# Rounding two weight blocks in turns, attention tiles between token-mixing products, and a block product moved behind the next group's first

## The chip, the core and the metric

The kernel runs on one core of a Trainium2 chip. The metric is the device time of one execution in microseconds (us). The kernel before takes 807.48 us (median of 3 runs, 807.12 to 807.95). The profiled execution has a span of 805.8 us from its first to its last instruction, at a granted TensorE clock of 0.999. All times inside a profile count from the start of that span.

The engines: TensorE (PE; PEld is its loading of weights), VectorE (DVE), ScalarE (ACT), GpSimd (POOL), and SyncE (SP), which issues the DMAs.

## The reference

```python
# attention: q, k, v are (8 batches, 8 heads, 576 tokens, 64)
kv  = einsum('bhsd,bhse->bhde', k, v)
o   = einsum('bhsd,bhde->bhse', q, kv)
x   = o / sqrt(mean(o*o, -1) + 1e-6) * g_norm       # RMS norm per head
x   = x.transpose(0, 2, 1, 3).reshape(8, 576, 512)  # heads side by side
# mixer
h   = relu(x^T @ w_tok1) @ w_tok2      # token mixing, 576 -> 256 -> 576
u   = x + h^T
out = u + relu(u @ w_ch1) @ w_ch2      # channel mixing, 512 -> 1536 -> 512
```

The mixer's weights are 64-bit floats in HBM. The kernel reads each as two 32-bit words and makes a rounded 32-bit float of it on the chip.

## The kernel before

It works in stages. Attention goes by pairs of batches (four pairs). Token mixing of one pair shares a stage with attention of the next, and both share it with the rounding of the weights:

- `start`: attention of pair 0 and the first token-mixing products
- `middle`: token mixing of pair 0, attention of pair 1
- `steady`, twice: token mixing of pair 1 and attention of pair 2, then of 2 and 3
- `last`: token mixing of pair 3
- then channel mixing, in nine groups of 512 rows (the ninth gathers the remainders), as block products in which sums of blocks take the place of one product. The first group (`channel1_once`, `channel2_once`) has wide products; the others have narrow ones in an order by places.

**Rounding of a block.** A block is fetched by a DMA and converted by ScalarE; six VectorE steps then follow, each on the result of the one before. "Step" in this text is one of these seven, from the conversion on.

```python
scale:  activation(dst, hi, Copy, scale=2**-112)                     # ScalarE, reads raw
clamp:  tensor_scalar(dst, dst, TOP, -TOP, min, max)                 # VectorE from here on
shift:  tensor_scalar(bits, bits, 3, logical_shift_left)
sign:   scalar_tensor_tensor(bits, raw[..., 1], 0x80000000, bits, bitwise_and, bitwise_or)
power:  tensor_scalar(part, bits, 0xFF800000, bitwise_and)
lower:  scalar_tensor_tensor(part, raw[..., 0], 2**-52, part, mult, mult)   # last use of raw
both:   dst = dst + part

def block(n, loads, dst):
    ...
    def fetch():                           # four buffers for raw
        raw.append(stage.tile([P, n, 2], U32, name="raw", tag="raw", bufs=4))
        for o, i in loads(raw[0]):
            dma(o, i)
    ...
    return (fetch,) + decode(dst, turn)    # decode returns the seven steps
```

**Attention of a pair.** A set is two tiles of 128 tokens; sets 0 and 1 belong to the first batch, 2 and 3 to the second, and 4 is the remainder of 64 tokens of each. A set takes both buffers of the pool `o`, so the next set starts when its gains and squares have read them.

```python
kv(side, half):    k^T v into ps["kv"]              # TensorE
evict(side, half): copy(kvp[side]..., ps_kv)        # ScalarE (VectorE for pair 0)
attend(c):         q^T kv into two tiles of ps["o"] # TensorE, set c
gain(c, h):        x = ps_o * g                     # VectorE
square(c, h):      sq = Square(ps_o)                # ScalarE
total(c, h):       tensor_reduce(ms, sq)            # VectorE
mean, sqrt, invert                                  # VectorE, ScalarE, VectorE (4 small steps)
scale(c, t):       eight activations x *= inv       # ScalarE
scale_pool(c, t):  tensor_mul(x, x, inv)            # GpSimd
```

**Token mixing of a pair.** Products h (`tok1`) fill four buffers of the pool `h`; the remainder's products end them; four relus on ScalarE free them; then nine tiles u (`tok2`) follow. Some u tiles are seeded: ScalarE copies x into the PSUM tile first, the products add to it, and ScalarE copies the result back. The others are added to x by VectorE.

**The stages as lists.** Each word is one step, and the order of the words is the order of issue, engine by engine: `kv`, `e` (evict), `l` (load), `a` (attend), `g` (gain), `q` (square), `t` (total), `m`, `r`, `i` (mean, sqrt, invert), `s` (scale), `p` (scale_pool), `h`, `hr`, `u`, `z` (seed), `lq` (load q), `w` (a token weight block's steps), `f` (fetch); a number is so many steps of the stream of channel weights.

```python
def steady(n0, n1):
    return [
        "kv00 l00 e00 1 -s40", "h00 3", "kv01 l01 e01 1", "h01 3", f"a0 q00 g01 q01 g00 {n0}",
        "h10 1 t00 t01 2", "h11 4", "hr 2 z2", "a1 q10 g11 q11 g10 1", "kv10 l10 e10 t10 t11 m0 r0 1",
        "u0 i0 1", "kv11 l11 e11", "u1 1 s00", "u2 z4 1", "a2 q20 g21 q21 g20", "u3 s01 t20 t21",
        "u4 z6 1", "a4 q40 g41 q41 g40 lq0", "u5 s10 t40 t41 1", "a3 q30 g31 q31 g30 lq1",
        "u6 s11 t30 t31 m2 r2 1 i2 p20 p21 s30", f"u7 1 s31 {n1}", "u8 2"]
```

The stream of channel weights, block after block, with the next block's conversion beside a block's fifth VectorE step and the fetch of the fourth next beside its sixth:

```python
def stream(blocks, ahead=4):
    steps = [blocks[0][1]]
    for n, block in enumerate(blocks):
        steps += block[2:]
        for at, m, k in ((-2, n + 1, 1), (-1, n + ahead, 0)):
            if m < len(blocks):
                steps[at] = do(lambda *fs: [f() for f in fs], steps[at], blocks[m][k])
    return iter(steps)
```

**From the first group to the second.** The first group's last steps, in the order of issue, are products 1, 6, 2, 7, 5, 4, 3 of `channel2_once`. In the second group's first block the products 1 and 6 stand at places 0 and 3, and between them ScalarE copies the result of product 1 (`read_first`). Before, two products without use stand around product 1:

```python
fetch_x(1, 0)
fetch_x(1, 1)
for place in range(2):
    t = late["c"].tile([P, DM], F32, name="ps_c")
    step = do(matmul, t[:, :FQ], lhsT=w_ch1[:, 0, 0, :P], rhs=w_ch1[:, 0, 0], start=True, stop=True)
    put(place, step) if place else step()
```

Of the kernel before, what the change touches and what calls it, by code (L numbers as in the profile page):

```python
# [11 lines left out]
F32 = mybir.dt.float32  # L12
# [7 lines left out]
def kernel(  # L20
# [33 lines left out]
    P = 128  # L54
    B, S, DM = k.shape
# [11 lines left out]
    FQ = FH // 2  # L67
# [31 lines left out]
    w_ch1 = consts.tile([P, 4, 4, FQ], F32, name="w_ch1")  # L99
# [6 lines left out]
    def do(f, *a, **kw):  # L106
        return lambda: f(*a, **kw)

    late = {}
# [4 lines left out]
    def dma(o, i, engine=nc.sync):  # L114
        keep(engine.dma_start(o, i))  # L115
# [10 lines left out]
    def matmul(*a, **kw):  # L126
        keep(nc.tensor.matmul(*a, **kw))  # L127
# [436 lines left out]
    def fetch_x(g, i):  # L564

        if g < NG:
            if i == 0:
                xg[g] = late["xg"].tile([P, J, DM], F32, name="xg")
            dma(xg[g][:, ts(i, 2)], u_dram[g].rearrange("(t p) e -> p t e", p=P)[:, ts(i, 2)])
# [11 lines left out]
    blocks, blocks_dram = {}, {}  # L581
# [37 lines left out]
    def m_psum(shape, name):  # L619
        return late["m"].tile(shape, F32, name=name, tag="m")  # L620
# [82 lines left out]
    def channel2_once(g):  # L703

        shape = [P, 2, DH]
        x = xg[g]
        quarter = lambda i, j: x[:, 2 * i:2 * i + 2, ts(j, DH)]

        def product(n, ps, start, stop):
            for p in range(2):  # L710
                for s in range(NS):
                    matmul(ps[:, p], lhsT=late["once"][n - 1][:, s, p], rhs=w2_of(n)[:, s],
                           start=(start and p == 0 and s == 0), stop=stop,
                           skip_group_check=True)

        p1, p6, p7, p5 = (m_psum(shape, f"ps_w{n}") for n in (1, 6, 7, 5))
        t1, u2, u3 = (r_tile() for _ in range(3))

        def first():
            product(1, p1, True, False)  # L720
            copy(t1, p1)

        def sixth():
            product(6, p6, True, True)
            tensor_add(u2, p6, t1)

        def seventh():
            product(7, p7, True, False)
            tensor_add(u3, p7, u2)
            tensor_add(quarter(0, 1), quarter(0, 1), u2)  # L730
            tensor_add(quarter(1, 0), quarter(1, 0), u2)

        def fifth():
            product(5, p5, True, False)
            tensor_add(u3, p5, u3)
            tensor_add(quarter(1, 1), quarter(1, 1), u3)

        def second():
            product(2, p1, False, True)
            tensor_add(quarter(0, 0), p1, quarter(0, 0))  # L740

        def fourth():
            product(4, p7, False, True)
            tensor_add(quarter(1, 0), p7, quarter(1, 0))
            store(g, xg, 1)

        def third():
            product(3, p5, False, True)
            tensor_add(quarter(0, 1), p5, quarter(0, 1))
            store(g, xg, 0)  # L750

        return [first, sixth, second, seventh, fifth, fourth, third]
# [7 lines left out]
    def put(place, *steps):  # L760
        beside[place] += steps

    def outer(place, size, mul, to, base=None, act=copy, onto=False):

        banks, t = {}, {}

        def product(n, name, start, stop):
            if start:
                banks[name] = m_psum([P, size], f"ps_{name}")
            mul(n, banks[name], start, stop)

        def temp(n, bufs):
            t[n] = late["tmp"].tile([P, FQ], F32, name=n, tag=n, bufs=bufs)[:, :size]
            t[n] = fit(t[n])
            return t[n]

        def fit(flat):
            return flat if size == P else flat.rearrange("p (w t) -> p w t", w=W)

        def read(o, i, j):

            if base:
                tensor_add(o, fit(banks["a"]), base(i, j))
            else:
                copy(o, fit(banks["a"]))

        def read_first():
            banks["c"] = late["c"].tile([P, DM], F32, name="ps_c")[:, :size]
            read(fit(banks["c"]), 0, 0)

        def write(i, j, name, n):
            tensor_add(to(i, j), fit(banks[name]), to(i, j) if onto else t[n])

        def put_on(i, j, n):
            if onto:
                tensor_add(to(i, j), to(i, j), t[n])  # L800

        def take(i, j, name, act):
            if onto:
                tensor_add(to(i, j), banks[name], to(i, j))
            else:
                act(to(i, j), fit(banks[name]))

        def at(n, name, start, stop, *steps):
            def all_of():
                product(n, name, start, stop)  # L810
                for step in steps:
                    step()

            products[place + PLACE[n]] = all_of

        at(1, "a", True, False, read_first)
        at(6, "a", False, False, lambda: read(temp("u2", 2), 0, 1))
        at(5, "b", True, False)
        at(7, "a", False, False, lambda: read(temp("u3", 1), 1, 1))
        at(2, "c", False, True, lambda: take(0, 0, "c", act))  # L820
        put(place + PLACE[7] + (1 if onto else 2), do(put_on, 1, 1, "u3"), do(write, 1, 1, "b", "u3"))
        at(4, "a", False, True, lambda: take(1, 0, "a", copy) if onto else read(to(1, 0), 1, 0))
        put(place + PLACE[4], do(put_on, 0, 1, "u2"))
        at(3, "b", False, True)
        put(place + PLACE[3] + 1, do(write, 0, 1, "b", "u2"))
# [213 lines left out]
    def weave(body, fill):  # L1039
        done = 0  # L1040
        for n, step in enumerate(body):
            step()
            upto = len(fill) * (n + 1) // len(body)
            while done < upto:
                fill[done]()
                done += 1

    def stream(blocks, ahead=4):


        steps = [blocks[0][1]]
        for n, block in enumerate(blocks):
            steps += block[2:]
            for at, m, k in ((-2, n + 1, 1), (-1, n + ahead, 0)):
                if m < len(blocks):
                    steps[at] = do(lambda *fs: [f() for f in fs], steps[at], blocks[m][k])
        return iter(steps)

    def play(lines, after={}, **stages):
# [38 lines left out]
    for block in tok1[2:] + tok2:  # L1098
# [5 lines left out]


    start = [
        "kv00 e00 l00 j14 w01 w11 w02 w03 w04 w05 w06 w07 w12 w13 w14 w15 w16 w17", "kv01 j10 e01 l01 f0",
        "a00 g00 q00", "a01 g01 q01 t00", "a10 g10 q10 t01 m0 r0", "a11 g11 q11 t10 i0 p00 p01",
        "kv10 j6 t11 m1 r1 e10 i1 s10 p11", "kv11 j2 e11", "h000 h001 h002 h003", "a20 g20 q20", "a21 g21 q21 t20",
        "h010 t21 m2 r2", "a30 g30 q30 i2 p20", "a31 g31 q31 t30", "h011 t31 m3 r3 p21", "a40 i3 p30 g40 q40 p31",  # L1110
        "h012 h013 t40 m4 r4 w21 i4 s40 lq0 l10 l11"]
    middle = [
        "kv00 e00 w31 w22 w23 w24", "h10 w25 w26 w27 f1 -lq1 l00 w32 w33 w34", "kv01 e01 l01 w41 w35 w36 w37",
        "h11 f2 w42 w43 w44", "hr w45 w46 w47 f3", "a0 q00 g01 q01 g00 t00 t01", "u0 z2 1", "u1 1",
        "a1 q10 g11 q11 g10 t10 t11 m0 r0", "u2 i0 1", "kv10 e10 z4 s00", "u3 1 s01", "kv11 e11 1",
        "u4 1 z6", "a2 q20 g21 q21 g20 s10", "u5 t20 t21 2", "a4 q40 g41 q41 g40 lq0 l10 l11", "u6 t40 t41 2",
        "a3 q30 g31 q31 g30 lq1 s11", "u7 t30 t31 m2 r2 1 i2 p20 p21 s30", "u8 1 s31"]

    def steady(n0, n1):
        return [  # L1120
            "kv00 l00 e00 1 -s40", "h00 3", "kv01 l01 e01 1", "h01 3", f"a0 q00 g01 q01 g00 {n0}",
            "h10 1 t00 t01 2", "h11 4", "hr 2 z2", "a1 q10 g11 q11 g10 1", "kv10 l10 e10 t10 t11 m0 r0 1",
            "u0 i0 1", "kv11 l11 e11", "u1 1 s00", "u2 z4 1", "a2 q20 g21 q21 g20", "u3 s01 t20 t21",
            "u4 z6 1", "a4 q40 g41 q41 g40 lq0", "u5 s10 t40 t41 1", "a3 q30 g31 q31 g30 lq1",
            "u6 s11 t30 t31 m2 r2 1 i2 p20 p21 s30", f"u7 1 s31 {n1}", "u8 2"]

    attentions = [attention(0, ((0,), (1,), (2,), (3,), (4,)))]
# [28 lines left out]
    first = ExitStack()  # L1156
# [47 lines left out]
    n = len(sums1) // 3  # L1204
# [8 lines left out]
             lambda: [f() for f in outer_u(1)], lambda: [f() for f in inner_u(1, 0, 7)]]  # L1213
    extra += [lambda: None] * (len(channel2_once_steps := channel2_once(0)) - len(extra))
    body = [step for pair in zip(channel2_once_steps, extra) for step in pair]
    weave(body, lasts + [f for fs, _ in inner2 for f in fs] + [f for _, f in inner1])
    fetch_x(1, 0)
    fetch_x(1, 1)


    for place in range(2):
        t = late["c"].tile([P, DM], F32, name="ps_c")
        step = do(matmul, t[:, :FQ], lhsT=w_ch1[:, 0, 0, :P], rhs=w_ch1[:, 0, 0], start=True, stop=True)
        put(place, step) if place else step()
    for n, (_, f) in enumerate(inner2):
        put(8 + n, f)
    for g in range(1, NG):
# [42 lines left out]
```

## Time and profile before

| Part of the profiled execution | number |
|---|---|
| span | 805.8 us |
| PE busy, share of the span | 788.6 us, 98% |
| PEld | 694.4 us, 86% |
| DVE | 683.3 us, 85% |
| ACT | 302.2 us, 38% |
| POOL | 79.6 us, 10% |
| DMA, mean over the span | 218 GB/s |
| first channel product (`ps_v`) starts | 200.17 us |
| second group's first product (`ps_a`) starts | 273.44 us |

A busy share is an average over stages with different limits, and the ends of matmuls are modelled, so a busy PE isn't PE at its peak. What a change is worth is read in the stage that it touches: which gaps the engine has there that sets the end, and what ended each of them. In the timeline, a number in brackets is the idle time before an instruction, with the engine and the tile that released it. Every product of 32-bit floats shows as two records in the profile, so a u tile of two products is "x4". Tiles are named for what they hold: `ps_o` and `ps_r` are sets and the remainder, `ps_h` and `ps_u` token mixing, `sq` squares, `raw` the fetched words, `w_ch` and `w_tok` weights.

### The profile page before, as it was taken

What the parts mean: (1) busy time and instruction counts of PE and PEld (TensorE: products, weight loads), DVE (VectorE), ACT (ScalarE), POOL (GpSimd) and SP (SyncE); (2) the same over time, 40 slices, a digit from 0 to 9 for tenths busy, and PEclk for the clock granted to TensorE, in tenths of its full rate; (3) what the DMA queues carried; (4) which work ended last, traced back from release to release, by engine and by line L of the source; (5) the groups of instructions that cost most, each with busy time, mean ns of one, the idle gap of its engine ahead of it and who ended that gap; (6) DMA issues with size and microseconds to landing.
All of it is one profiled execution on the core that took longest, in us unless ns stands there. A gap on an engine that the chain in (4) does not pass through costs nothing.

```text
span 805.8 us, 17651 instructions
## 1 busy us (share of the span) xinstructions
PE 788.6 (98%) x7012; PEld 694.4 (86%) x7012; DVE 683.3 (85%) x1308; ACT 302.2 (38%) x838; POOL 79.6 (10%) x75
## 2 busy tenths in 40 slices
PE   6999999999999999999999999999999999999997
PEld 6645554544888899999999999999999999999997
DVE  4688989999886978978987997997898899799687
ACT  1357585664110134234234234332424423423331
POOL 1210101010000011012003003001101200300300
PEclk9999999999999999999999999999999999999999
DMA  9999998436458567468467648738836855863642
GB/s 289 320 345 351 334 354 304 158 119 208 150 175 294 194 210 239 131 221 267 149 201 240 201 153 259 234 118 262 265 119 217 262 166 181 250 201 123 218 147 83
DMA packets 97346, 175.51 MB, mean 218 GB/s; under 512 B 7024, under 2 KB 54128, under 8 KB 97264
## 3 DMA queue, kind: packets, MB, share of 16 engines
q1 hardware_dynamic: 95584, 172.65, 66.6%
q10 hardware_dynamic: 1680, 1.74, 0.7%
q8 instruction: 55, 0.90, 0.5%
q14 instruction: 27, 0.22, 0.1%
HBM read 137.79 MB, written 36.57 MB: 216 GB/s over the span
## 4 chain that ended last, share of the span: by engine, by line
PE 83%; DVE 6%; DMA 5%; ACT 3%; SPq 1%; issue 1%; ACTq 0%; DVEq 0%
PE ps_a L127 37%; PE ps_b L127 19%; PE ps_c L127 9%; PE ps_v L127 5%; PE ps_w L127 4%; PE ps_u L127 4%; DMA v_in<-in_v_dram 3%; PE ps_h L127 2%; ACT x L475 1%; SPq L115 1%; DMA raw<-in_moe_w_ch_dram 1%; DMA k_in<-in_k_dram 1%; DVE ms L442 1%; DVE part L187 1%; DVE x L421 1%; PE ps_o L127 1%
## 5 line engine op out<-in xcount | busy, mean ns | idle before, releaser
L124 ACT COPY u<-ps_a 128x128 f32<-128x128 f32 (+1 forms) x160 | 56.1, 351 | 156.6 <-PE ps_a L127 156.6
L118 POOL TENSOR_TENSOR v<-v,v 128x384 f32<-128x384 f32 (+1 forms) x48 | 61.4, 1301 | 532.8 <-ACT v L124 492.8
L127 PE MATMUL ps_b<-uT,sums 128*128 128x128 f32 x672 | 86.2, 276 | 0.0
L127 PEld LDWEIGHTS ps_b<-uT,sums 128*128 128x128 f32 x672 | 80.7, 192 | 0.2
L118 DVE TENSOR_TENSOR v<-v,v 128x768 f32<-128x768 f32 (+1 forms) x86 | 79.5, 932 | 1.1
L127 PE MATMUL ps_a<-uT,w_ch 128*128 128x128 f32 x576 | 78.9, 275 | 0.0
L124 ACT COPY ps_c<-ps_a 128x128 f32<-128x128 f32 (+1 forms) x80 | 26.9, 336 | 129.5 <-PE ps_a L127 129.5
L118 DVE TENSOR_TENSOR v<-ps_b,u 128x384 f32<-128x384 f32 x112 | 61.5, 549 | 12.3 <-PE ps_b L127 10.6
L127 PEld LDWEIGHTS ps_a<-uT,w_ch 128*128 128x128 f32 x576 | 71.4, 192 | 0.4
L127 PE MATMUL ps_u<-h,w_tok 128*128 128x512 f32 (+1 forms) x160 | 68.0, 608 | 1.6 <-ACT h L121 0.6
L127 PE MATMUL ps_h<-x,w_tok 128*128 128x512 f32 (+1 forms) x160 | 65.9, 604 | 0.0
L118 DVE TENSOR_TENSOR uT<-uT 128x512 f32<-128x512 f32 (+4 forms) x103 | 63.1, 629 | 0.8
L127 PE MATMUL ps_a<-uT,w 128*128 128x128 f32 x432 | 60.0, 275 | 0.0
L127 PEld LDWEIGHTS ps_a<-uT,w 128*128 128x128 f32 x432 | 54.0, 192 | 0.0
L127 PEld LDWEIGHTS ps_h<-x,w_tok 128*128 128x128 f32 (+1 forms) x160 | 25.9, 189 | 31.1 <-issue 28.3
L127 PEld LDWEIGHTS ps_u<-h,w_tok 128*128 128x128 f32 (+1 forms) x160 | 24.5, 178 | 31.9 <-issue 24.9
L121 ACT ACTIVATE v<-v 128x384 f32<-128x384 f32 (+1 forms) x86 | 42.5, 528 | 23.0 <-DVE v L118 22.5
L118 DVE TENSOR_TENSOR sv<-v 128x384 f32<-128x384 f32 x80 | 43.4, 551 | 8.9 <-ACT v L121 8.9
L118 DVE TENSOR_TENSOR xg<-xg,r 128x512 f32<-128x512 f32 x74 | 50.0, 686 | 0.7
L475 ACT ACTIVATE x<-x,inv 128x64 f32<-128x64 f32 x184 | 46.0, 336 | 9.6 <-DVE inv L461 9.6
L127 PE MATMUL ps_a<-sums,sv 128*128 128x128 f32 x336 | 47.1, 276 | 0.0
L127 PE MATMUL ps_a<-uT,sums 128*128 128x128 f32 x336 | 46.8, 275 | 0.0
(134 smaller groups left out, 1576.5 us busy)
## 6 DMA issues: line engine op xcount, KB each, us to landing
sums<-sums SPq DMA_DIRECT2D x112, 576.0 KB, 4.4
qT<-in_q_dram SPq DMA_DIRECT2D x8, 1152.0 KB, 9.6
xt<-u_dram SPq DMA_DIRECT2D x36, 256.0 KB, 4.0
blocks<-y SPq DMA_DIRECT2D x72, 128.0 KB, 2.7
uT<-blocks SPq DMA_DIRECT2D x36, 256.0 KB, 4.9
xg<-u_dram SPq DMA_DIRECT2D x18, 512.0 KB, 5.1
k_in<-in_k_dram SPq DMA_DIRECT2D x16, 512.0 KB, 9.2
u_dram<-x SPq DMA_DIRECT2D x16, 512.0 KB, 4.9
```

What stands on the lines that cost most here:

```text
L115: keep(engine.dma_start(o, i))
L118: keep(engine.tensor_tensor(out=o, in0=a, in1=b, op=op))
L121: keep(nc.scalar.activation(o, a, AF.Relu))
L124: keep(nc.scalar.copy(o, a))
L127: keep(nc.tensor.matmul(*a, **kw))
L187: keep(nc.vector.scalar_tensor_tensor(out=part[0], in0=raw()[..., 0], scalar=2.0 ** -52, in1=part[0], op0=ALU.mult, op1=ALU.mult))
L421: keep(nc.vector.tensor_mul(x, bank[c, h], g_sb.to_broadcast([P, number(c), D])))
L442: keep(nc.vector.tensor_reduce(stats_of(c)[0][:, h], sq[c, h], axis=AX.X, op=ALU.add))
L475: keep(nc.scalar.activation(x[:, k, h], x[:, k, h], AF.Copy, scale=inv[:, k, h]))
```

## The change

It has three parts. Rounding goes through two blocks in turns: three steps of one block alternate with three of the block before, so that neighbours don't depend on each other, and the conversions and fetches get other places. In the steady stages, the second set of attention moves from behind the h products to between them; the tiles u and the remainder are regrouped, and the seeds and scalings move with them. Then the first group's last block product moves behind the second group's first product, in the place of the two products without use, and two of the first group's four PSUM tiles come from another pool.

```diff
-        p1, p6, p7, p5 = (m_psum(shape, f"ps_w{n}") for n in (1, 6, 7, 5))
+        p1, p6 = (m_psum(shape, f"ps_w{n}") for n in (1, 6))
+        p7, p5 = (late["c"].tile(shape, F32, name="ps_c", tag="c") for _ in range(2))
@@
-            banks["c"] = late["c"].tile([P, DM], F32, name="ps_c")[:, :size]
+            banks["c"] = late["c"].tile([P, DM], F32, name="ps_c", tag="c")[:, :size]
@@ def stream(blocks, ahead=4):
+        def all_of(*fs):
+            return do(lambda: [f() for f in fs])
         steps = [blocks[0][1]]
-        for n, block in enumerate(blocks):
-            steps += block[2:]
-            for at, m, k in ((-2, n + 1, 1), (-1, n + ahead, 0)):
-                if m < len(blocks):
-                    steps[at] = do(lambda *fs: [f() for f in fs], steps[at], blocks[m][k])
+        second = [None] * 3
+        for n in range(len(blocks) + 1):
+            first = list(blocks[n][2:5]) if n < len(blocks) else [None] * 3
+            if n + 1 < len(blocks):
+                first[1] = all_of(first[1], blocks[n + 1][1])
+            if second[1] and n - 1 + ahead < len(blocks):
+                second[1] = all_of(second[1], blocks[n - 1 + ahead][0])
+            steps += [f for pair in zip(first, second) for f in pair if f]
+            second = list(blocks[n][5:8]) if n < len(blocks) else second
         return iter(steps)
@@ start
-        "kv00 e00 l00 j14 w01 w11 w02 w03 w04 w05 w06 w07 w12 w13 w14 w15 w16 w17", "kv01 j10 e01 l01 f0",
+        "kv00 e00 l00 j14 w01 w11 w02 w03 w04 w12 w05 w13 w06 w14 w07 w15 w16 w17", "kv01 j10 e01 l01 f0",
@@ middle
-        "kv00 e00 w31 w22 w23 w24", "h10 w25 w26 w27 f1 -lq1 l00 w32 w33 w34", "kv01 e01 l01 w41 w35 w36 w37",
-        "h11 f2 w42 w43 w44", "hr w45 w46 w47 f3", "a0 q00 g01 q01 g00 t00 t01", "u0 z2 1", "u1 1",
-        "a1 q10 g11 q11 g10 t10 t11 m0 r0", "u2 i0 1", "kv10 e10 z4 s00", "u3 1 s01", "kv11 e11 1",
-        "u4 1 z6", "a2 q20 g21 q21 g20 s10", "u5 t20 t21 2", "a4 q40 g41 q41 g40 lq0 l10 l11", "u6 t40 t41 2",
-        "a3 q30 g31 q31 g30 lq1 s11", "u7 t30 t31 m2 r2 1 i2 p20 p21 s30", "u8 1 s31"]
+        "kv00 e00 w31 w22 w23 w24", "h10 w41 w25 w32 w26 w33 w27 w34 f1 -lq1 l00", "kv01 e01 l01 w35 w42 w36 w43",
+        "h11 w37 w44 f2", "hr w45 w46 w47 f3", "a0 q00 g01 q01 g00 t00 t01", "u0 z2 1", "u1 1",
+        "a1 q10 g11 q11 g10 t10 t11 m0 r0", "u2 i0 1", "kv10 e10 z4 s00 p10", "u3 1 s01", "kv11 e11 z6 1",
+        "u4", "a2 q20 g21 q21 g20 s11", "u5 t20 t21 1", "a4 q40 g41 q41 g40 lq0 l10 l11", "u6 t40 t41 3",
+        "a3 q30 g31 q31 g30 lq1", "u7 t30 t31 m2 r2 2 i2 p20 p21 s30", "u8 1 s31"]
@@ def steady(n0, n1):
-            "h10 1 t00 t01 2", "h11 4", "hr 2 z2", "a1 q10 g11 q11 g10 1", "kv10 l10 e10 t10 t11 m0 r0 1",
-            "u0 i0 1", "kv11 l11 e11", "u1 1 s00", "u2 z4 1", "a2 q20 g21 q21 g20", "u3 s01 t20 t21",
-            "u4 z6 1", "a4 q40 g41 q41 g40 lq0", "u5 s10 t40 t41 1", "a3 q30 g31 q31 g30 lq1",
+            "h10 t00 t01 3", "a1 q10 g11 q11 g10", "h11 t10 t11 m0 r0 3", "hr i0 2",
+            "kv10 l10 e10 1", "kv11 l11 e11 z2", "u0 s00 1", "u1 2", "a2 q20 g21 q21 g20", "u2 s01 z4 t20 t21 1",
+            "u3 1", "a4 q40 g41 q41 g40 lq0", "u4 s10 t40 t41 z6 1", "u5 1", "a3 q30 g31 q31 g30 lq1",
@@ first group to second
     body = [step for pair in zip(channel2_once_steps, extra) for step in pair]
+    behind = body.pop(-2)
     weave(body, lasts + [f for fs, _ in inner2 for f in fs] + [f for _, f in inner1])
-    fetch_x(1, 0)
-    fetch_x(1, 1)
-    for place in range(2):
-        t = late["c"].tile([P, DM], F32, name="ps_c")
-        step = do(matmul, t[:, :FQ], lhsT=w_ch1[:, 0, 0, :P], rhs=w_ch1[:, 0, 0], start=True, stop=True)
-        put(place, step) if place else step()
+    put(0, behind, do(fetch_x, 1, 0), do(fetch_x, 1, 1))
```

## The prediction

> **What bounds the kernel now.** I read the busy lines first, then the engines by windows, then the timelines of single engines around each gap of TensorE. The windows give start and end in us, length, then busy us (and instructions) of PE, PEld, DVE, ACT and POOL, the clock, the DMA share and GB/s:
>
> ```profile
> 80.00:100.00 20.00, 20.00 (x220) 10.02 (x216) 19.34 (x28) 9.77 (x31) 2.79 (x2) 1.00 1.08 336
> 180.00:200.00 20.00, 20.00 (x54) 7.92 (x52) 19.73 (x24) 9.17 (x17) 0.00 (x0) 1.00 0.64 197
> 300.00:500.00 200.00, 200.00 (x1790) 199.93 (x1789) 173.07 (x353) 69.58 (x194) 23.39 (x19) 1.00 0.66 207
> ```
>
> Behind 200 us, three quarters of the span, TensorE is packed (the answer on waits names none for PE behind 290 us), so all that comes before it shifts the end one for one. In the attention and token mixing stages, up to 200 us, TensorE and VectorE are both nearly full, and up to 137 us the DMA is too (37.38 MB from 30 to 140 us, 340 GB/s). The change can earn only TensorE's gaps. The timeline of TensorE shows the four largest ones of the stages that are changed; the number in brackets is the idle time and what ended it:
>
> ```profile
> 54.75 2.81 PE L127 MATMUL ps_u<-h,w_tok 128*128 128x512 f32 x6 [0.55 <-DVE w_tok L118]
> ...
> 74.24 1.16 PE L127 MATMUL ps_o<-kvp,qT 64*64 64x64 f32 x64 [1.33 <-ACT sq L425]
> ...
> 101.97 1.98 PE L127 MATMUL ps_u<-h,w_tok 128*128 128x512 f32 x4 [0.57 <-ACT h L121]
> ...
> 161.93 1.16 PE L127 MATMUL ps_o<-kvp,qT 64*64 64x64 f32 x64 [1.12 <-ACT sq L425]
> ```
>
> With small ones (0.04, 0.21, 0.2, 0.26, 0.1) all gaps from 54 us on sum to 4.4 us. The kernel's first TensorE instruction of each pair's stage (kv00) starts at 40.18 (middle), 79.01 (steady one), 123.38 (steady two), and the last stage at 168.52 us.
>
> The timeline of VectorE shows what a dependence costs. Columns: start, duration:
>
> ```profile
> 96.46 0.55 DVE L166 TENSOR_SCALAR w_ch<-w_ch 128x768 f32<-128x768 f32 x1
> 97.05 0.56 DVE L170 TENSOR_SCALAR w_ch<-w_ch 128x768 uint32<-128x768 uint32 x1
> ...
> 101.10 0.55 DVE L166 TENSOR_SCALAR w_ch<-w_ch 128x768 f32<-128x768 f32 x1
> 101.57 0.68 DVE L421 TENSOR_TENSOR x<-ps_o,g_sb 128x512 f32<-128x512 f32 x1
> ```
>
> The same clamp holds VectorE 0.59 us when the next one reads its result, 0.47 when it doesn't: 0.12 us for each neighbouring pair of dependent steps.
>
> [...] the last rounding step takes 1.70 us at 83.19, beside GpSimd's scaling (81.28 to 84.07), and 0.96 elsewhere. [...]
>
> **The change, part by part.**
>
> *Rounding in turns.* Each stage of a pair has some 15 neighbouring dependent pairs before (counted in the timeline from 123 to 168 us) and next to none after: 15 x 0.12 = 1.8 us of VectorE in each steady stage, 9 x 0.12 = 1.1 in the last. No PE gap is VectorE's throughput as such, so this only shortens lags. For the token weights (44 to 54.6 us) the interleave gains under 0.2 us: VectorE's first step of the next block stands before the old block's last two and must wait for ScalarE (46.95 us).
>
> *Price: raw words are needed earlier.* Fetch of a block stays at nearly the same step, but its first conversion (ScalarE) moves 5 steps forward. In before the sixth block already stalls ScalarE. Its timeline:
>
> ```profile
> 91.39 0.92 ACT L163 ACTIVATE w_ch<-raw 128x768 f32<-128x768 f32 x1
> 100.00 0.94 ACT L163 ACTIVATE w_ch<-raw 128x768 f32<-128x768 f32 x1 [7.70 <-DMA raw<-in_moe_w_ch_dram]
> 100.84 2.05 ACT L121 ACTIVATE h<-ps_h 128x512 f32<-128x512 f32 x4
> ```
>
> The DMA is full and the same bytes are queued ahead of that block, so I expect it at about 100 us again.
>
> *Middle.* One rounding step less (0.9 us) stands ahead of the remainder tile's gains, and the third set's wait of 1.33 goes; but a conversion (0.8 us) now stands ahead of the eviction that the second side's first set needs, so that set starts some 0.7 late. One scaling (eight ScalarE instructions, 1.9 us) goes to GpSimd, about 1 us there by the rows at 37.44 and 40.91 (two in 2.04), which only lightens ScalarE where TensorE doesn't wait for it. By its steps this stage ends 0.7 to 0.8 us earlier: steady one begins at 78.2.
>
> *Steady one.* From 78.2, by TensorE's own times (kv 1.3, h 3.63, set 1.09, h with remainder 5.35), the second set now stands between two h products, at 92.7 to 93.8, and TensorE reaches the first u at 101.7. But ScalarE now has the sixth block's conversion ahead of that set's squares, and the relus behind those. From 100.0: conversion 0.84, first square 0.6, gain 0.6, two reductions 1.2, mean 0.1 and turn 0.1, root 0.2, two relus 1.1: u can start at 104.8, a wait of **3.1 us**. The second kv product, worth 1.3, is done by then, and was not before.
> VectorE, stopped from 96.7 to 101.4, is late for the third set (ends 109.5): its gains end 3.1 us after it. ScalarE's second square waits for the first gain, then copy 0.48, eight scalings 1.92 and the seed 0.48 stand before u4; TensorE has only two u tiles and the remainder (4.3 us) meanwhile: wait 3.1 + 0.5 + 2.9 - 4.3 = **2.2**. From 104.8: u 3.63, set 1.09, u 3.63, remainder 0.65, wait 2.2, u 3.63, set 1.09, u 5.4: 126.2, against 123.38.
>
> *Steady two.* DMA is no longer full. The set that waited 1.12 now has two u tiles ahead of it: that wait goes, and 0.36 of small ones. VectorE's lag at the third set comes to 2.4, so the seed of u4 makes TensorE wait 2.4 + 0.5 + 2.9 - 4.3 = 1.5. Of work alone the stage is 42.9, so it takes 44.4 against 45.2: the last stage begins at 170.6 against 168.6, **+2.0**. There TensorE works 31.6 us without waits; VectorE's 1.1 keep it ahead.
>
> *Boundary to the second group.* Timeline of TensorE and its weight loads:
>
> ```profile
> 272.79 0.81 PE L127 MATMUL ps_c<-w_ch 128*128 128x384 f32 x2
> ...
> 274.11 0.81 PE L127 MATMUL ps_c<-w_ch 128*128 128x384 f32 x2
> ...
> 274.82 0.74 PEld L127 LDWEIGHTS ps_a<-uT,sums 128*128 128x128 f32 x6 [0.52 <-ACT ps_c L124]
> ```
>
> The two products only fill time, 0.65 and 0.71 us; both go. The block product of 5.13 us covers the copy that they covered. But that copy needs a buffer whose last reader on VectorE ends at 272.7 before and some 0.5 later now: about 0.3 back here, 0.3 at the next block: **-0.8**.
>
> Sum: +2.0 - 0.8 = +1.2, so 808.7 if the sixth block lands at 100 us and all queues go as above.
>
> **Rivals.** *The raw words don't stop it.* If they came 4 us earlier, u would start at 101.8, VectorE's lag would be 1.4 and the seed's wait 0.5: steady one ends at 121.5, steady two gives 0.8, the boundary 0.8: -3.5, so 804.0. For it: the change takes the waits one by one as if tuned to a trace. Against: the bytes ahead are the same, and the DMA share is 1.08.
> *VectorE is what counts.* If the lags drop more than I count (1.8 us a stage), the waits on seeds vanish: another 2 to 3 us less, toward 802 to 803 with the first rival. Against: VectorE itself waited for ScalarE or TensorE in the same stages.
> *Nothing moves.* The gaps close, open again elsewhere, and only the boundary's 0.8 stay: 806.7.
>
> **Range and chances.** I give the stall seven chances in ten (about +1.2, give or take 1.5) and the rivals three (-1 to -4.5). I put the point a little below the stall's sum: 808.0, eight in ten from 803.6 to 810.0. All gaps together are 4.4 + 1.4 = 5.8 us, 0.7%, so a gain of over 2% can't come from here, and a loss of 16 us would need waits five times what I count.
>
> **What would show it.** In the timeline of ScalarE after, a conversion released by the raw DMA near 100 us, the second set's squares behind it; in that of TensorE a wait of about 3 us at the first u of steady one on the relus, waits of 1 to 2 us on seeds (ps_u on ACT) near 114 and 158, none on squares at the last set; kv00 of steady two near 126, block product next to ps_a without filler near 268 to 274. If ScalarE never waits for raw near 90 to 100, my sum is wrong by 4 us and the first rival holds. If steady two starts before 123, it fell.

## The result, and the profile after

The changed kernel takes 811.0 us (median; 810.49 to 811.27) against 807.3 of the kernel before (806.82 to 807.95): a ratio of 1.0045, 95% interval 1.0027 to 1.0062. It is slower by 3.7 us where 808.0 was predicted, and lies outside the range of 803.6 to 810.0. The profiled executions show 808.7 against 805.8 us, of which 3.9 us are lost before 200 us (the first channel product starts at 204.08 instead of 200.17) and 1.0 won back behind it.

The timeline of TensorE in the changed kernel, its larger gaps and the first kv product of each steady stage (start, duration, and in brackets the idle time before with what ended it):

```profile
73.88 1.16 PE L127 MATMUL ps_o<-kvp,qT 64*64 64x64 f32 x64 [0.71 <-ACT sq L425]
...
78.66 1.33 PE L127 MATMUL ps_kv<-v_in,k_in 128*64 128x64 f32 x40
...
89.34 0.93 PE L127 MATMUL ps_o<-kvp,qT 64*64 64x64 f32 x48 [0.39 <-ACT kvp L124]
...
105.24 5.32 PE L127 MATMUL ps_u<-h,w_tok 128*128 128x512 f32 x8 [2.22 <-ACT h L121]
...
116.77 3.70 PE L127 MATMUL ps_u<-h,w_tok 128*128 128x512 f32 x8 [0.86 <-ACT ps_u L124]
...
127.28 1.33 PE L127 MATMUL ps_kv<-v_in,k_in 128*64 128x64 f32 x40
...
161.83 3.70 PE L127 MATMUL ps_u<-h,w_tok 128*128 128x512 f32 x8 [1.81 <-ACT ps_u L124]
```

Left out are 0.26 at 67.80 (set 2 on a kv eviction) and 0.32 at 121.88 and 166.94 (the seeds of u6). The gaps from 54 us on now sum to 7.4 us, against 4.0 by the same count before. The predicted waits are there: the first u on the relus, the seed of u4 in both steady stages, none on squares in steady two. In middle, where the wait on squares was to go, 0.71 of it stayed. Compare the durations, too: eight u records take 3.70 us at 116.77 and **5.32 at 105.24**. The windows of the same stretch say why. Behind the busy times (and instructions) of PE, PEld, DVE, ACT and POOL their last three numbers are the granted clock, the DMA share and GB/s; the third from the end is the one to read.

```profile
104.00:105.00 1.00, 0.00 (x0) 0.00 (x0) 1.00 (x2) 1.00 (x3) 0.00 (x0) 1.00 1.08 428
105.00:106.00 1.00, 0.76 (x1) 0.50 (x2) 1.00 (x2) 1.00 (x3) 0.00 (x0) 0.56 0.96 372
106.00:107.00 1.00, 1.00 (x2) 0.33 (x1) 0.90 (x5) 1.00 (x4) 0.00 (x0) 0.50 1.00 368
...
108.00:109.00 1.00, 1.00 (x3) 0.49 (x2) 1.00 (x3) 1.00 (x6) 0.00 (x0) 0.73 1.09 326
```

TensorE idles for 2.2 us, and then its granted clock is half for more than 3 us (0.56, 0.50, 0.50 and 0.73 in the four windows from 105 to 109 us). That was in no step of the prediction. The mean clock of the whole span, 0.998, hides it (the kernel before has 0.999).

The cause of the idle time stands in the timeline of ScalarE, and one engine further in that of VectorE:

```profile
100.42 0.92 ACT L163 ACTIVATE w_ch<-raw 128x768 f32<-128x768 f32 x1 [8.67 <-DMA raw<-in_moe_w_ch_dram]
101.24 1.07 ACT L425 ACTIVATE sq<-ps_o 128x512 f32<-128x512 f32 x2
103.99 0.23 ACT L452 ACTIVATE root<-ms 128x32 f32<-128x32 f32 x1 [1.68 <-DVE ms L447]
104.12 2.04 ACT L121 ACTIVATE h<-ps_h 128x512 f32<-128x512 f32 x4
```

```profile
101.86 0.69 DVE L421 TENSOR_TENSOR x<-ps_o,g_sb 128x512 f32<-128x512 f32 x1 [4.36 <-ACT sq L425]
102.47 1.27 DVE L442 TENSOR_REDUCE ms<-sq 128x8 f32<-128x512 f32 x2
```

The sixth block's conversion waits for its raw words until 100.42; set 1's squares, the gain that they release, two reductions, the root and the relus follow one after another, and TensorE comes last. This is the predicted chain, link by link; only the wait at its end, 2.22 us, is shorter than the 3.1 worked out, because TensorE reached u at 103.0 and not at 101.7.

At the boundary to the second group (timeline of TensorE) the product stands where it was meant to, at the small price of a wait of 0.23:

```profile
271.53 0.83 PE L127 MATMUL ps_a<-uT,w_ch 128*128 128x128 f32 x6
272.19 5.35 PE L127 MATMUL ps_c<-w_ch,v 128*128 128x256 f32 x24
277.77 0.94 PE L127 MATMUL ps_a<-uT,sums 128*128 128x128 f32 x6 [0.23 <-ACT ps_c L124]
```

### The profile page after: what moved, and what is told of

It reads as the page before. It is cut to its first block, busy times and chain, and to the rows that moved or that the text cites. A ratio compares the mean times of both kernels' runs of the same rounds, so it can differ in the third digit from the quotient of the medians.

```text
span 808.7 us, 17645 instructions
## 1 busy us (share of the span) xinstructions
PE 788.1 (97%) x7008; PEld 694.0 (86%) x7008; DVE 678.6 (84%) x1308; ACT 300.2 (37%) x830; POOL 80.3 (10%) x76
## 4 chain that ended last, share of the span: by engine, by line
PE 84%; DVE 7%; ACT 4%; DMA 3%; issue 1%; SPq 1%; ACTq 0%; DVEq 0%
PE ps_a L127 37%; PE ps_b L127 19%; PE ps_c L127 10%; PE ps_u L127 5%; PE ps_v L127 5%; PE ps_h L127 4%; ACT x L475 2%; PE ps_w L127 2%; DVE x L421 1%; DVE ms L442 1%; DMA raw<-in_moe_w_ch_dram 1%; PE ps_kv L127 1%; PE ps_o L127 1%; DMA k_in<-in_k_dram 1%; PE ps_j L127 1%
## 5 line engine op out<-in xcount | busy, mean ns | idle before, releaser
L127 PE MATMUL ps_a<-sums,v 128*128 128x128 f32 x336 | 46.7, 275 | 0.0
```

## The experiments

Fifteen kernels were compared, counting before and after; each of the others was timed in five rounds beside the kernel before, whose median was 807.1 to 807.5.

| Kernel | what it is | us | ratio to before (95%) |
|---|---|---|---|
| bound | before + boundary | 806.47 | 0.9989 (0.9982 to 0.9996) |
| turns | before + rounding in turns, start, middle | 813.44 | 1.0072 (1.0059 to 1.0085) |
| sets | before + new steady lists | 809.78 | 1.0024 (1.0015 to 1.0033) |
| conv6 | after, sixth conversion later | 807.60 | 1.0005 (0.9996 to 1.0015) |
| fetch6 | after, sixth fetch ahead of k and v | 807.60 | 1.0008 (1.0000 to 1.0016) |
| warm | after + products in the wait | 811.00 | 1.0048 (1.0036 to 1.0060) |
| seeds | after, seeds ahead of scalings | 805.89 | 0.9985 (0.9978 to 0.9991) |
| seedswarm | seeds + products in the wait | 805.97 | 0.9982 (0.9973 to 0.9991) |
| early | conv6 + seeds | 803.34 | 0.9957 (0.9945 to 0.9969) |
| plain | early without rounding in turns | 803.71 | 0.9961 (0.9949 to 0.9974) |
| early2 | early + kv evictions earlier | 803.88 | 0.9964 (0.9950 to 0.9979) |
| early3 | early + seventh conversion later | 803.83 | 0.9957 (0.9944 to 0.9971) |
| early4 | early3 + kv evictions earlier | **802.48** | 0.9945 (0.9932 to 0.9957) |

### The three parts by themselves

```diff
# bound: of the change's diff, the hunks on p7, p5, tag="c" and "first group to second"
# turns: of the change's diff, the hunks on stream, start and middle
# sets:  of the change's diff, the hunk on steady
```

> The kernel before with the third part of the change alone: the first group's last block product behind the next group's first, the two products without use gone, two PSUM tiles from the other pool. Theory R (the loss comes from the sixth weight block's conversion, which stops ScalarE in steady one): this part gains what I counted, 0.8 us, so some 806.5 us. Rival P (the moved product or the smaller pool costs): 808 us or more.

Measured: −1.0 us, as theory R and the prediction's last step have it. Rival P is out: the boundary is no part of the loss.

> The kernel before with rounding in turns and the new lists of start and middle, but with its own lists of the steady stages and its own boundary. The sixth conversion again waits for its raw words until about 100 us, but here the relus and not set 1's squares stand behind it. Theory R: the first u waits about 1 us on relus instead of 0.57, TensorE's clock stays up, and what middle gains (0.35) pays for it: 807 to 808 us. Rival V (the order of the sets costs, whatever rounding does): the same 807. Rival F (rounding in turns costs by itself, by its fetches and conversions everywhere): 810 or more.

Measured: 813.44, over 5 us more than theory R allowed. The timeline of ScalarE in turns shows what I had missed:

```profile
99.66 0.91 ACT L163 ACTIVATE w_ch<-raw 128x768 f32<-128x768 f32 x1 [7.91 <-DMA raw<-in_moe_w_ch_dram]
...
105.31 0.90 ACT L163 ACTIVATE w_ch<-raw 128x768 f32<-128x768 f32 x1 [2.79 <-DMA raw<-in_moe_w_ch_dram]
...
107.60 0.26 ACT L124 COPY kvp<-ps_kv 128x128 f32<-128x128 f32 x1
110.25 0.23 ACT L452 ACTIVATE root<-ms 128x32 f32<-128x32 f32 x1 [2.39 <-DVE ms L447]
110.38 0.25 ACT L124 COPY kvp<-ps_kv 128x128 f32<-128x128 f32 x1
```

The sixth conversion waits, with only the relus behind it, and TensorE waits for nothing there. But the *seventh* waits as well, and in the old lists a seed, set 1's squares, the root and both kv evictions stand behind it; the second eviction starts at 110.38, where the kernel before has it at 106.67. TensorE then waits for a kv eviction and for a seed (timeline of TensorE in turns):

```profile
110.68 0.93 PE L127 MATMUL ps_o<-kvp,qT 64*64 64x64 f32 x48 [1.56 <-ACT kvp L124]
...
115.83 2.44 PE L127 MATMUL ps_u<-h,w_tok 128*128 128x512 f32 x4 [2.12 <-ACT ps_u L124]
```

and behind that the granted clock falls to 0.50 (118 to 120 us): its four u records take 2.44 instead of 1.98. So the mechanism holds, but not for one block alone: here the seventh conversion, moved forward, stops what stands behind it on ScalarE. Rival F, that rounding in turns costs by its conversions, named the size better than I did.

> The kernel before with the new lists of the steady stages alone: the second set between the h products, the seeds behind the scalings, rounding one block after another. The sixth conversion stands five steps later, behind set 1's squares. Theory R: no wait above 1 us at the first u of steady one and no lower clock there; the seeds of u4 cost about 1 us in each steady stage, the wait of 1.12 before the last set goes: 807 to 808 us. Rival V: 810 or more, without rounding in turns.

Measured: 809.78, above theory R's 807 to 808. There is no stop at the first u, as R expected. The timeline of TensorE shows where the rest is:

```profile
112.66 3.70 PE L127 MATMUL ps_u<-h,w_tok 128*128 128x512 f32 x8 [0.99 <-ACT ps_u L124]
...
158.62 5.26 PE L127 MATMUL ps_u<-h,w_tok 128*128 128x512 f32 x8 [2.17 <-ACT ps_u L124]
```

The seed of u4 costs 0.99 and 2.17 us, and behind the longer wait the eight records take 5.26 us: the granted clock was 0.50 from 159 to 161 us. In the changed kernel, with rounding in turns, the second of these waits is 1.81. The new lists alone carry a fault of their own, the seeds behind eight scalings.

The three parts don't add: −1.0 + 6.0 + 2.3 is 7.3, the change measures 3.7. Two of the costs aren't in the profile of the changed kernel: set 2 of steady one doesn't wait there for a kv eviction (1.56 us in turns), as TensorE has eight u records ahead of it, and the clock doesn't fall at u4 of steady two (1.6 us in sets).

### The stop at the sixth conversion

```diff
# conv6: in stream
-            if n + 1 < len(blocks):
+            if n + 1 == 5:
+                second[2] = all_of(second[2], blocks[n + 1][1])
+            elif n + 1 < len(blocks):
                 first[1] = all_of(first[1], blocks[n + 1][1])
```

> The changed kernel with the sixth block's conversion alone three steps later, behind set 1's squares; VectorE's order is as in the changed kernel. Theory R: the first u of steady one starts at about 103.0 instead of 105.24, its eight records take 3.6 us instead of 5.25, the seed of u4 comes sooner: 806.2 to 807.2 us. Rival V: the wait at u only moves to the seeds, 809.5 or more. Rival P: 811, as without the edit.

Measured: 807.60, 3.4 us less than the changed kernel and 0.4 above theory R's range. ScalarE in conv6, then TensorE:

```profile
99.58 0.23 ACT L452 ACTIVATE root<-ms 128x32 f32<-128x32 f32 x1 [1.35 <-DVE ms L447]
100.15 0.94 ACT L163 ACTIVATE w_ch<-raw 128x768 f32<-128x768 f32 x1 [0.34 <-DMA raw<-in_moe_w_ch_dram]
```

```profile
103.00 3.70 PE L127 MATMUL ps_u<-h,w_tok 128*128 128x512 f32 x8
107.18 1.16 PE L127 MATMUL ps_o<-kvp,qT 64*64 64x64 f32 x64 [0.48 <-ACT kvp L124]
...
113.61 3.70 PE L127 MATMUL ps_u<-h,w_tok 128*128 128x512 f32 x8 [1.01 <-ACT ps_u L124]
```

The words land at 100.15 as ever, but set 1's squares and root stand ahead of the conversion now, and only the relus behind it: u starts at 103.00 without a gap, and its eight records take 3.70 us. Set 2 now waits 0.48 for a kv eviction behind the seventh conversion, and the seed of u4 1.01; u4 starts 3.2 us earlier than in the changed kernel. The stop is thus worth about 3.4 us, and this is shown, not argued: VectorE's instructions and their order are the same in both.

```diff
# fetch6: in steady; l00 loads k and v of the next pair
-            "kv00 l00 e00 1 -s40", "h00 3", ...
+            "kv00 e00 1 -s40", "h00 1 l00 2", ...
```

> The changed kernel with the sixth block's fetch ahead of the first four k and v transfers (1.1 MB) of the steady stages instead of behind them; conversions and all else stay. Theory Q (the conversion's wait is set by the fetch's place in the queue of transfers, which is 9 us deep at 340 GB/s): the raw words land 3 us sooner, near 97, the first u of steady one waits for next to nothing, the clock stays up: 807 to 808 us, as with the conversion moved. Rival (the buffer of raw words or the full DMA holds it wherever it stands): 810.5 to 811.5.

Measured: 807.60, theory Q. The queue of SyncE shows the sixth block's fetch at 91.41 in the changed kernel (first line) and, in fetch6, ahead of the k and v transfers (second and third line); ScalarE's conversion in fetch6 is the fourth:

```profile
91.41 0.53 SPq L115 DMA_DIRECT2D raw<-in_moe_w_ch_dram  x1
...
85.77 0.34 SPq L115 DMA_DIRECT2D raw<-in_moe_w_ch_dram  x1
86.21 2.35 SPq L115 DMA_DIRECT2D k_in<-in_k_dram  x2
...
95.83 0.93 ACT L163 ACTIVATE w_ch<-raw 128x768 f32<-128x768 f32 x1 [4.37 <-DMA raw<-in_moe_w_ch_dram]
```

The conversion starts at 95.83 instead of 100.42, and the first u, at 102.67, no longer waits. From the fetch's issue to the conversion it takes 9.0 us in one kernel and 10.1 in the other: what the edit changes is the issue, 5.6 us earlier. The DMA is as full as before (a share of 0.85 over the first 200 us, 0.84 in the changed kernel), but *which* bytes come first is a choice of the list. Two edits that share nothing else remove the same 3.4 us.

### The clock

```diff
# warm: in steady one only, between kv11 and u0
+    o = ps["o"].tile([P, DM], F32, name="ps_j", tag="o")
+    for _ in range(3):
+        matmul(o[:, :P], lhsT=ident, rhs=ident, start=True, stop=True)
```

> The changed kernel with three products of the unit matrix with itself, of no use, on TensorE between the second kv product and the first u of steady one, where it waits 2.22 us for the relus. They leave the wait but shorten its idle part by some 1.6 us. Theory K (the idle TensorE lost its granted clock, and the first eight u records ran at half of it): u starts at 105.2 as before, its eight records take 3.6 to 3.7 us instead of 5.25, 809.2 to 809.7 us. Rival (these records are slow for what they read, as VectorE and the DMA are busy too): 5.2 us again, 811 us.

TensorE in warm:

```profile
103.05 0.94 PE L127 MATMUL ps_j<-ident 128*128 128x128 f32 x6
105.33 3.70 PE L127 MATMUL ps_u<-h,w_tok 128*128 128x512 f32 x8 [1.34 <-ACT h L121]
...
116.63 3.70 PE L127 MATMUL ps_u<-h,w_tok 128*128 128x512 f32 x8 [2.17 <-ACT ps_u L124]
```

It is the clock that makes these records slow, and not what they read: u starts at the same time, reads the same data beside like traffic (a DMA share of 0.97 from 105 to 106 us and 1.07 from 106 to 107, against 0.96 and 1.00), and takes 3.70 us at a granted clock of 1.00. But the time is 811.0 again, and theory K's 809.2 to 809.7 is missed. Nearly all of the 1.6 us comes back at the next wait: the seed of u4 is ready when it is ready (116.63 against 116.77), so TensorE, earlier now, waits 2.17 instead of 0.86. And in this execution the clock fell in steady two instead, to 0.50 from 163 to 166 us, behind the seed's wait of 1.82 (eight records in 5.40 us at 161.69); it is one of the slower of the six executions, which range from 809.8 to 813.2.

To see the clock without that seed, the products were put into seeds (below):

> As seeds (the changed kernel with the seeds ahead of the scalings), with the three products without use of warm ahead of the first u of steady one. In seeds that u waits 1.91 us and its eight records take 5.40 us at half the granted clock; no wait stands behind them to give a gain back, as the seed of u4 did in warm. Theory K (the lower clock costs the end its 1.7 us where nothing behind hides it, in most executions): the records take 3.7 us, 804.2 to 804.8 us. If the clock falls in few executions only, or VectorE behind it sets the end anyway: 805.6 to 806.2, as seeds.

Measured: 805.97, the same as seeds. Its profile has the clock at 1.00 in all stages up to 200 us and eight u records in 3.70 us at the first u, where the profile of seeds has a clock of 0.50 from 106 to 108 us and 5.40 us; in the median the products earned nothing. The single executions of seeds suggest why: the four with a mean clock of 0.997 took 807.3 to 808.2 us, the 18 others (0.998 and more) 804.8 to 806.9; the profiled one, with the fall, was among the four. If the other three fell at the same place, a fall costs about 2 us where little behind hides it, and in that kernel it is the exception. That is an inference: the mean also counts half the clock behind the last product, which stands at the end of the span in the profiles of before (0.50 from 805.0 us on) and after (0.50 from 808.5 on).

### The seeds, and both repairs

```diff
# seeds: in steady
-            ... "u2 s01 z4 t20 t21 1", ... "u4 s10 t40 t41 z6 1", ...
+            ... "u2 z4 s01 t20 t21 1", ... "u4 z6 s10 t40 t41 1", ...
```

> The changed kernel with two words exchanged in each steady stage: the seeds of u4 and u6 stand ahead of the eight scalings instead of behind them, 1.9 us earlier on ScalarE. The stop at the sixth conversion stays. Theory S (the seeds' waits come from that order): the waits of 0.86 and 1.81 at u4 and twice 0.32 at u6 go; nothing else takes their place but some tenths: 807.5 to 808.7 us. Rival V (VectorE's lag holds the sets, so the wait reappears at a set or the remainder): 810 or more.

Measured: 805.89, 1.6 us below theory S's range. TensorE in seeds, the first u of steady one and the seeded u4 of both steady stages:

```profile
104.94 5.40 PE L127 MATMUL ps_u<-h,w_tok 128*128 128x512 f32 x8 [1.91 <-ACT h L121]
...
115.62 3.70 PE L127 MATMUL ps_u<-h,w_tok 128*128 128x512 f32 x8
...
158.40 3.70 PE L127 MATMUL ps_u<-h,w_tok 128*128 128x512 f32 x8
```

All four seed waits (3.3 us in the changed kernel) are gone and nothing took their place; in the steady stages only set 0 (0.40) and the first u still wait. The profiled execution is 2.8 us shorter than that of the changed kernel, which fits theory S. The median gains 5.1; the rest would be the half clock at the first u, on which theory S counted and which most executions of this kernel don't seem to have (above). Rival V is out.

> Both repairs on the changed kernel: the sixth conversion three steps later, and the seeds ahead of the scalings. Of 807.6 us with the first alone, the waits at seeds are 1.01, 1.81 and twice 0.32. If they add up freely: 804.2 us, in 803.7 to 805.2. If VectorE holds the sets: 806 or more.

Measured: 803.34, ratio 0.9957 (0.9945 to 0.9969), 0.4 us below the range expected. The two repairs together give 7.7 us, and the result is 4 us faster than the kernel before. In its timeline TensorE shows no gap of 0.15 us or more behind set 0 of steady one (0.39 at 88.99) up to the channel stage.

> All of early without rounding in turns: the stream, start and middle of the kernel before, the new steady lists with the seeds ahead of the scalings, and the new boundary. Its sixth conversion stands behind set 1's squares by itself. If rounding in turns is worth only some tenths of lag here (theory R), this runs like early, 803.3 us, plus what the middle stage lost by going back (steady one begins some 0.3 later): 803.3 to 804.5 us. If the turns' 1.8 us of VectorE a stage are needed by the new order of sets: 805.5 or more.

Measured: 803.71 against early's 803.34; the intervals overlap. Once no conversion stops ScalarE, rounding in turns with its lists of start and middle is worth 0.4 us, which this measurement can't tell from nothing. VectorE's busy time, 683.3 us before, fell to 678.6 in the changed kernel; next to none of it reaches the end.

```diff
# early2: on early
-            "kv00 l00 e00 1 -s40", "h00 3", "kv01 l01 e01 1", ...      # steady
+            "kv00 l00 e00 1", "h00 3", "kv01 l01 e01 1 -s40", ...
-        ... "u3 1 s01", "kv11 e11 z6 1", ...                           # middle
+        ... "u3 1", "kv11 e11 s01 z6 1", ...
# early3: on early, seventh conversion as well
-            if n + 1 == 5:
+            if n + 1 in (5, 6):
# early4: both
```

> As early, and in middle and the steady stages the kv evictions stand ahead of eight scalings, too, for which sets 2 (middle) and 0 (steady one) waited 0.26 and 0.38 us. If those two go: 0.5 to 0.6 us less than early. Where another wait takes their place (squares of the last set in middle), less than 0.3.

Measured: 803.88, no gain; 802.58 to 806.47, and the profiled execution is the slowest. The waits of 0.26 and 0.38 are gone, so TensorE comes to set 2 sooner, and meets the seventh conversion:

```profile
106.87 0.91 ACT L163 ACTIVATE w_ch<-raw 128x768 f32<-128x768 f32 x1 [3.64 <-DMA raw<-in_moe_w_ch_dram]
107.68 0.42 ACT L124 COPY kvp<-ps_kv 128x128 f32<-128x128 f32 x2
```

That is ScalarE; TensorE's set 2 waits 1.98 us for these copies and then runs at half clock (0.60 from 108 to 109 us, 0.50 from 109 to 111; 1.84 us instead of 1.16). A gain of half a us ahead of a transfer that doesn't move was no gain here.

> The changed kernel with the seeds ahead of the scalings and both the sixth and the seventh conversion three steps later (early has the sixth alone), so that the second side's kv evictions no longer stand behind the raw words of the seventh. TensorE had no gap there in early, so 803.3 us as early, give or take 0.4.

> As early3, and the kv evictions of middle and of the steady stages' first side ahead of eight scalings, as in early2. In early2 those waits went, but set 2 of steady one then waited 1.98 us for a kv eviction behind the seventh conversion and the clock fell. With that conversion behind the evictions: 0.5 us less than early3, 802.6 to 803.2 us. If it is early2's median again, 803.9, the wait came from something else.

Measured: 803.83 and 802.48. The seventh conversion behind the evictions does nothing by itself, as expected. With the evictions early it lets their gain through, and more: 1.35 us less than early3 where 0.5 was expected. The gaps that went account for 0.6 of it; the rest isn't explained. Early4 runs from 802.25 to 803.08 us, early3 from 803.38 to 804.37. Early4 has a ratio of 0.9945 (0.9932 to 0.9957), is 4.6 us faster than the kernel before and 8.5 faster than the change as it was made. Steady one, with gaps of 2.22 + 0.86 + 0.32 + 0.39 us and the half clock in the changed kernel, has none of 0.15 us here; the first u and set 2 in the timeline of TensorE in early4, 3.7 us earlier than u was at 105.24:

```profile
101.54 3.70 PE L127 MATMUL ps_u<-h,w_tok 128*128 128x512 f32 x8
105.17 1.16 PE L127 MATMUL ps_o<-kvp,qT 64*64 64x64 f32 x64
```

## Why the prediction was wrong, point by point

The main mechanism was right and the sum too small. The steps that failed are the waits in middle and the two steady stages. By the profile these stages end 1.8 us later than worked out, and two terms make up most of that: the seeds behind eight scalings cost some 1.2 us more than their term (u4 came 0.3 us late in each stage, and the 0.32 at u6 had no term), and middle won 0.35 us instead of 0.8, with 0.71 left of the wait on squares that was to go; the cause of that stays open. The seeds experiment shows the first as a cause: with the seeds ahead of the scalings all these waits go.

- **The main step held.** The sixth block's conversion was released by the raw DMA at 100.42 ("I expect it at about 100 us again"), set 1's squares, gain, root and relus came behind it, and u started at 105.24 where 104.8 was worked out. conv6 and fetch6 show it to be the cause of 3.4 us.
- **Middle: a term too large.** "Steady one begins at 78.2": it began at 78.66. The shorter list was credited in full, but the last set still waits 0.71 for the remainder's second square, where its wait of 1.33 was to vanish. In VectorE's order that square's gain still stands behind two reductions and a rounding step. Set 2 waits 0.26 for a kv eviction behind sixteen scalings, less than the 0.7 predicted. Early2 and early4 take that wait away, and the last set's stays at 0.7, so it has another cause, which no run isolates. In steady one a kv eviction behind scalings costs set 0 0.39, which no step had; there it only shortens the wait at the first u.
- **Steady one: a term missing, another too large.** The stage took 48.6 us, 48.0 was worked out, so it looks nearly right; it wasn't. The half clock behind the stop (5.32 instead of 3.70 us, 1.6) was missing. The seed of u4 was given 2.2 and cost 0.86, because TensorE came to it late. The two errors hide each other, and warm shows it: with the clock up, the seed's wait was 2.17, the predicted 2.2, and u4 started only 0.14 us earlier. So the half clock hardly cost the changed kernel anything here. What is left of the stage's 0.6 is u4, 0.3 late counted from the stage's start, and the seed of u6, 0.32.
- **Steady two: the step that failed in size.** "44.4 against 45.2": it took 45.16. The set's wait of 1.12 went, as predicted. The seed of u4 cost 1.81 where 1.5 was worked out, and the seed of u6 another 0.32 in each stage, which the sum didn't have. I had followed one seed behind eight scalings and not the next one, with the same order.
- **Boundary: right.** −0.8 was worked out; bound measures −1.0, and the profiles show 1.0 won back behind 200 us.
- **The sum.** +0.45 in middle, +0.6 and +0.8 in the steady stages make the last stage begin at 172.44 instead of 170.6. In the profile the end is then +2.9 where +1.2 was the sum. The medians differ by 3.7; the other 0.8 lie between the two profiled executions (807.63 and 810.49) and the medians, within the spread of single executions (0.8 us and more).
- **The choice of the point failed.** The sum gave 808.7; I went down to 808.0 and set the upper end at 810.0 for rivals of which none came. The first ("the raw words don't stop it") was stated against the evidence that I had shown myself. The second (VectorE counts) fell too: the waits on seeds stayed, and plain shows that turns are worth next to nothing once the seeds stand ahead. The range up was 1.3 us over a sum whose three stage terms missed by 0.45, 0.6 and 0.8 us, all in the same direction.
- **A premise was narrower than I put it.** "The DMA is full and the same bytes are queued ahead" is true of this change, but not a property of a full DMA: fetch6 lands the words 4.6 us earlier by the order of issue.

## What to carry to other kernels

When a change moves work forward on an engine that keeps the order of its list, as ScalarE did here (set 1's squares at 101.24 us, behind the conversion that got its words at 100.42), list for each moved instruction what it waits for and all that now stands behind it; follow it for every block and not just for the first: here an engine freed at one stop came sooner to the next (in early2 TensorE then waited 1.98 us). In this kernel it paid to put a conversion that waits for a transfer behind what other engines wait for (3.4 us), and a seed that a matmul needs ahead of work that is wanted later (5.1 us). A gap of some two microseconds of TensorE, as here, is to be priced with the half clock that followed it in six of the profiled executions (1.6 us on eight u records in the changed kernel), and with what stands behind to hide it.

## What was not expected of the hardware

**The clock fell after gaps of some 2 us.** In the profiled executions it fell to 0.50 behind idle times of 1.82 (warm), 1.91 (seeds), 1.98 (early2), 2.12 (turns), 2.17 (sets) and 2.22 us (after), and not behind 1.34 (warm), 1.56 (turns), 1.81 (after, conv6), 1.82 (fetch6) and 2.17 (warm, at 116.63). So the length alone doesn't decide: here gaps of 1.8 to 2.2 us went either way. In the changed kernel it then stayed at half for a little over 3 us (105 to 109 us, above): 1.6 us lost on eight records of 128x512. What decides beside the length is not shown here.

**Dependence between VectorE neighbours.** This one was expected from the trace before, and held: in the changed kernel the interleaved steps follow each other every 0.47 us (power at 88.18, shift at 88.65, the next at 89.12), where the dependent pair took 0.59 in the trace before. That it bought next to nothing is a matter of the path.
